# Loading and scaling the last segment's rows some slots sooner in both attention stages, and the second transform's last rows later

## The chip, the cores and the metric

The kernel runs on one core of a Trainium2 chip. The metric is the device time of one execution in microseconds (us). A core has a matrix engine (PE, TensorE), a vector engine (DVE), an activation engine (ACT), a general engine (POOL, GpSimd) and a queue engine (SP) that issues most DMA transfers. Each engine works through its own list of instructions in order; semaphores make one engine wait for another.

## The reference

Four layers follow each other on an activation of 2048 rows by 512 columns, each with a layer norm ahead of it and its result added to the row stream: a Fourier transform, an attention, the same Fourier transform, the same attention.

```python
x = A_x
x = x + _A_ref(_layernorm(x), dft_seq_re, dft_seq_im, dft_hid_re, dft_hid_im)
x = x + _B_ref(_layernorm(x), wq, wk, wv, wo, beta)
x = x + _A_ref(_layernorm(x), dft_seq_re, dft_seq_im, dft_hid_re, dft_hid_im)
x = x + _B_ref(_layernorm(x), wq, wk, wv, wo, beta)
```

`_layernorm` takes from each row its mean and divides by the root of its variance. `_A_ref` multiplies the rows by the DFT matrices along the hidden dimension and along the sequence, and keeps the real part. `_B_ref` has 32 heads of 16 columns and cuts the 2048 rows into 4 segments of 512; within a segment it is causal softmax attention, and earlier segments come in through a running memory that is read with the queries of a segment and updated with its keys and values.

## The kernel before

Rows are handled in 16 tiles of 128 (`NT`), four to a segment (`LT`), and segment `s` of an attention stage has tiles 4s to 4s+3. Four stages are laid out one behind the other on one axis of numbered slots: transform one at `a1`, attention one at `b1`, transform two at `a2`, attention two at `b2`. Every piece of work is a Python generator, and `place(order, gen, slots)` (L184) says in which slots its next step is traced; within a slot the steps go by `order` and then by the order in which they were placed. That trace is the program order.

PE instructions keep the program order (`in_order`, L78), and so do those wrapped in `pin`. For DVE, ACT, POOL and SP a planner makes each engine's list when the kernel is built: it steps through a modelled time and takes the earliest in program order among what it holds to be ready, so a later step can be drawn ahead into a gap. The row maxima of the scores (L827) are marked more urgent than their place. `behind_max` (L161) keeps an instruction behind the maximum that was traced last.

Layer norm of a tile is a chain over three engines. `moments` (L130) takes mean and variance on DVE (bn_stats L132, bn_aggr L133), `inverse_roots` (L140) adds epsilon on DVE (L143) and raises to the power -0.5 on POOL (L145), `row_scale` (L148) refines that in four small DVE instructions (L150 to L153), and `normal` (L164) makes the scaled rows `xn` on DVE (L166). For most tiles the statistics are taken by the stage that makes the rows (`measure`, L199). Only the last segment's tiles 12 to 15 lack them, so the next stage must take them itself.

In an attention stage `prep` (L679) handles two tiles. Its steps are: load the two tiles (L680); for the last segment, take the statistics up to the POOL power (L685); for the last segment `row_scale` (L688), and `xn` of the first tile; four PE transposes of the first tile into `xnT` and the split of the result into `xT` (L695 to L699); `xn` of the second tile; its transposes. The segment's first pair is placed round the slot b-60 and its second round b-55 (L1190), where b is the segment's first slot. A unit of attention (four heads of one segment) takes ten slots, and a segment 80. In the same slots PE computes the scores of a unit (`nat` for the maxima, `sT` for the softmax, `pv_bank` with the values), projections (`pqk`, `pvv`) and the output product of an earlier segment (`po`).

In transform two, `normalise` (L210) handles two tiles in three steps at t-8, t-3 and t (L601): load; statistics, for tiles 12 to 15 alone; `row_scale`, `xn`, and the split of `xn` into `xa` on ACT (L96) and DVE (L98). The slots t stand in the list at L1250. PE multiplies `xa` with blocks of the DFT matrix, and each block (a "right") must be split too: `one_right` (L338) by one ACT and one DVE pass into a tile `chi` or `clo`, of which there are three each, four slots before its product; some blocks are first added to another on DVE (L444, L457). A product step is six matmuls in one slot. The second transform runs products P1 and P7 for two slots a step up to slot a2+56, then P7, P2 and P4 for three slots a step up to a2+80. Tiles 12 to 15 are first used from a2+69 on. `negate` (L642) writes `minus`, the sign-changed row scales of all 16 tiles, for `add_rows` (L253), which scales and adds rows for the last products from slot a2+80 on.

Tiles loaded by `load_rows` share five buffers (`xt`, L119) and the `xn` tiles two. SP issues the loads in its own list, among the block fetches, the stack loads of the units and the writes of results.

Of the kernel before, what the change touches and what calls it, by code (L numbers as in the profile page):

```python
# [14 lines left out]
ALU = mybir.AluOpType  # L15
# [6 lines left out]
NSEG = 4  # L22
L = S // NSEG
NT = S // P
DT = D // P
TC = S // 512
LT = L // P
# [29 lines left out]
def spectral_infini_kernel(  # L57
# [13 lines left out]
    V, A, G, T = nc.vector, nc.scalar, nc.gpsimd, nc.tensor  # L71
# [46 lines left out]
    def load_rows(src, name="xt"):  # L118
        t = sb.tile([P, 512], F32, name=name, tag="xt", bufs=5)  # L119
        nc.sync.dma_start(t, src)  # L120
        return t
# [26 lines left out]
    def row_scale(rr, ve, r):  # L148
        t = sb.tile([P, LT], F32, name="rt", bufs=2)[:, : rr.shape[1]]
        V.tensor_tensor(out=t, in0=r, in1=r, op=ALU.mult)  # L150
        V.tensor_tensor(out=t, in0=t, in1=ve, op=ALU.mult)
        V.tensor_scalar(t, t, -0.5, 1.5, op0=ALU.mult, op1=ALU.add)
        V.tensor_mul(rr, r, t)  # L153
# [30 lines left out]
    def place(order, gen, *at):  # L184
        for t in itertools.chain(*at):
            slots.setdefault(t, []).append((order, gen))

    def run_from(t, n, step=1):
        return range(t, t + n * step, step)
# [6 lines left out]
    row_r = consts.tile([P, NT], F32, name="row_r")  # L196
    minus = consts.tile([P, NT], F32, name="minus")
# [7 lines left out]
    def place_spectral(x_in, x_out, t0, end, ln_at, direct):  # L205
# [396 lines left out]
        t = start  # L602
        if direct:
            place(2, contract(0), run_from(t, 4 * HALF, 2))
            for k in range(HALF):
                place(3, read_plain(0, k), [t + 8 * k + d for d in (-12, -4, 1, 4)])
                place(3, change_rows(k), [t + 8 * k + d for d in (5, 9)])
            t += 8 * HALF
            names = "P1", "P2", "P7", "P4"
            for tcn in range(1, TC):  # L610
                for n, name in enumerate(names):
                    place(2, product(tcn, name), run_from(t + n, HALF, 4))
                for k in range(HALF):
                    place(3, read_all(tcn, k), [t + 4 * k + d for d in (-11, -6, -4, -2, -1)])
                t += 4 * HALF
            for k in range(HALF):
                place(3, join_rows(k), [t + 5 * k + d for d in (-33, -27)])
            for tcn in range(1, TC):
                for n, name in enumerate(CHAIN):
                    place(2, product(tcn, name), run_from(t + n, HALF, 3))  # L620
                for k in range(0, HALF, 2):
                    place(3, read_rest(tcn, k), [t + 3 * k + d for d in (-12, -6, -3, 0)])
                t += 3 * HALF
        else:
            SOLO = 1
            phases = [(("P1",), range(SOLO)), (("P1", "P7"), range(SOLO, TC)), (("P7", "P2", "P4"), range(SOLO)), (("P2", "P4"), range(SOLO, TC))]
            for names, tcns in phases:
                n = len(names)
                for tcn in tcns:
                    for j, name in enumerate(names):  # L630
                        place(2, product(tcn, name), run_from(t + j, HALF, n))
                    for k in range(HALF):
                        u = t + n * k
                        if n == 1:
                            place(3, read_one(tcn, k, "P1"), [u - 9, u - 4])
                        else:
                            first = n - 2
                            if first:
                                place(3, read_added(tcn, k), [u + d for d in (-10, -6, -4)])
                            place(3, read_pair(tcn, k, names[first:]), [u + first + d for d in (-10, -6, -4, -3)])  # L640
                    t += n * HALF
            def negate():  # L642
                V.tensor_scalar(minus, row_r, -1.0, None, op0=ALU.mult)
                yield

            place(3, negate(), [t - 50])
            for k in range(HALF):
                place(3, add_rows(k), [t - 48 + 6 * k, t - 44 + 6 * k])
            for tcns in (0, 1), (2, 3):
                at = {tcn: [] for tcn in tcns}  # L650
                for name, tcn in itertools.product(CHAIN, tcns):
                    at[tcn] += run_from(t, HALF)
                    for k in range(HALF):
                        place(3, read_one(tcn, k, name), [t + k + d for d in (-9, -4)])
                    t += HALF
                for tcn in tcns:
                    place(2, chained(tcn), at[tcn])
        for k in range(2 * DT):
            cc, d = k // DT, k % DT
            tag = "craw" if k < 2 else ("chi", "clo")[k % 2]  # L660
            t = end - 7 + k if k < 2 else end - 3 + (k - 2) // 2
# [13 lines left out]
    def place_attention(x_in, x_out, t0, w_at, out_at):  # L675
# [3 lines left out]
        def prep(s, n):  # L679
            xt = [load_rows(x_in[s * LT + i]) for i in n]  # L680
            yield
            mine = slice(s * LT + n[0], s * LT + n[-1] + 1)
            mv, rr = row_mv[:, mine], row_r[:, mine]
            if s == NSEG - 1:
                ve, r = row_stats(xt, mv)  # L685
            yield
            if s == NSEG - 1:
                row_scale(rr, ve, r)  # L688
            for j, i in enumerate(n):
                with behind_max():  # L690
                    xn = normal(xt[j], mv[:, j], rr[:, j : j + 1])
                yield
                if i == 0:
                    xT[s] = sb.tile([P, 2, DT, 512], F32R, name="xT", bufs=1)
                pt = bank("xnT", (P, DT, P))  # L695
                for d in range(DT):
                    T.transpose(pt[:, d], xn[:, d * P : (d + 1) * P], ident)
                sl = slice(i * P, (i + 1) * P)
                split(xT[s][:, 0, :, sl], xT[s][:, 1, :, sl], pt)  # L699
                if j + 1 < len(n):  # L700
                    yield
            yield
# [477 lines left out]
        for n in range(NSEG * USEG):  # L1180
            t = t0 + SU * n
# [5 lines left out]
        for s in range(NSEG):  # L1187
            b = t0 + SS * s
            for j in range(2):
                t = b - (43, 51, 60, 60)[s] + 5 * j  # L1190
                first = (8, 5, 3)
                place(2, prep(s, (2 * j, 2 * j + 1)), [*(t - d for d in first), t, t, t + 2])
            place(2, values(s), *([light(b - 20), light(b)] if s else [run_from(b - 18, 8), light(b - 10)]))
            place(2, alloc_out(s), [b - 13])
            o = b + SS
            if s < NSEG - 1:
                free = light(o + 20) + light(o + 40) if s < NSEG - 2 else run_from(o + 20, DT * LT, 3)
            else:
                free = [out_at(k) for k in range(4 * LT)]
            if s == NSEG - 1 and x_out is out_tiles:  # L1200
                for i in range(LT):
                    place(2, outproj_split(s, i), [o - 12 + i], range(o - 7 + 3 * i, o - 7 + 3 * i + 3) if i < LT - 1 else (o + 2, o + 4, o + 4), [o + 5 + 1, o + 7])
                place(1.5, transpose_last(s), [o + 5])
            else:
                for i in range(LT):
                    at = free[DT * i : DT * (i + 1)]
                    place(2, transpose_out(s, i), [at[0] - 4 - i % 2])
                    place(2, outproj(s, i), at)
            for g in range(NG):
                t = b + SG * g  # L1210
                late = [] if s or g > 1 else [b + 3 + 2 * g]
                at = {
                    (0, 0): run_from(b - 34, 8),
                    (0, 1): run_from(b - 26, 8),
                    (0, 2): among(b, b + 13, 8),
                    (0, 3): among(b + 13, b + 29, 8),
                    (1, 0): among(b - 40, b - 29, 8),
                    (1, 1): among(b - 29, b - 17, 8),
                }.get((s, g), light(t - 50))
                place(2, proj(s, g, "q"), at[:4], post(at[3]))  # L1220
                place(2, proj(s, g, "k"), at[4:], post(at[7]), late)
                if s > 0:
                    place(2, mem_read(s, g), [t - 12, t - 8])
                if s < NSEG - 1:
                    place(2, mem_update(s, g), [t + 6, t + 9] if g else [t + 16, t + 19])
# [10 lines left out]
    a2 = b1 + LB - 18  # L1236
    b2 = a2 + TC * 7 * HALF + LEAD

    def w_at(b):
# [7 lines left out]
    place_attention(mids[0], mids[1], b1, w_at(b1), lambda k: b1 + LB + 11 + k // 2)  # L1247
    place_spectral(
        mids[1], mids[2], a2, b2 - LEAD,
        [((2 * j, 2 * j + 1), a2 + t) for j, t in enumerate((-40, -24, -8, 2, 24, 34, 46, 54))],  # L1250
        False,
    )
    place_attention(mids[2], out_tiles, b2, w_at(b2), lambda k: b2 + LB + 8 + k)
# [83 lines left out]
```

## Time and profile before

| | |
|---|---|
| median of 3 runs | 1813.44 us (1812.06 to 1814.43) |
| profiled execution | 1812.16 us, span of its instructions 1810.4 us |
| PE busy | 1745.1 us, 96% of the span, 10192 matmuls |
| DVE busy | 1404.3 us, 78% |
| ACT busy | 1116.3 us, 62% |
| POOL busy | 475.7 us, 26% |
| mean granted PE clock | 0.994 of full speed |

Busy time is the time in which an engine has an instruction in work, and a matmul's end is modelled. A timeline row gives start, duration, engine, line, operation, output and inputs; where the engine sat idle before it, the idle time and what ended it stand in brackets at the end. Nearly all PE instructions have the line of one helper (L82), so they are told apart by the name of what they write. A row of time slices gives the busy time of PE, PE's weight loads, DVE, ACT and POOL in that slice, with the number of instructions in parentheses, and after them the granted PE clock (1.00 is full speed), the DMA share and GB/s.

### The profile page before, as it was taken

Reading aid. Unit: us, or ns where it says so; the run is one execution under the profiler, and the core shown is the slowest. Engines: PE = TensorE matmul, PEld = TensorE weight load, DVE = VectorE, ACT = ScalarE, POOL = GpSimd, SP = SyncE. Lnnn points to the kernel's source line nnn. Section 1 sums busy time; section 2 is a strip of 40 time slices with the busy share of each in tenths; the row PEclk is TensorE's granted clock in tenths of the full one; section 3 lists DMA queues with packets and bytes.
Section 4 is the critical chain, followed back from the end, with each engine's and each line's share of the span. In section 5 each row is a group of like instructions: output and inputs, shape, how many; then the busy total and the mean of one; then the engine's idle time right before and its main releaser. Section 6 shows DMA issues by size and latency. Waiting matters only on the chain.

```text
span 1810.4 us, 32184 instructions
## 1 busy us (share of the span) xinstructions
PE 1745.1 (96%) x10192; PEld 1260.2 (70%) x10192; DVE 1404.3 (78%) x4233; ACT 1116.3 (62%) x2391; POOL 475.7 (26%) x797
## 2 busy tenths in 40 slices
PE   7999999999999999999999999999998999999998
PEld 6888777877556666665578788888875666666654
DVE  8888987764877878878877997667658788787785
ACT  3334443432877878778764765444338887867785
POOL 1000000013443445355520000000134443534442
PEclk9999999999999999999999999999999999999999
DMA  8787765355443543444566876644545344344341
GB/s 279 245 274 236 249 228 169 116 168 175 137 151 108 156 127 123 138 127 132 164 205 203 275 231 221 195 147 153 170 136 179 124 138 144 116 138 139 103 130 42
DMA packets 169498, 302.81 MB, mean 167 GB/s; under 512 B 19568, under 2 KB 70768, under 8 KB 169328
## 3 DMA queue, kind: packets, MB, share of 16 engines
q1 hardware_dynamic: 159152, 287.39, 50.0%
q10 hardware_dynamic: 10176, 13.37, 2.0%
q8 instruction: 80, 1.31, 0.3%
q14 instruction: 90, 0.74, 0.1%
HBM read 211.83 MB, written 88.08 MB: 166 GB/s over the span
## 4 chain that ended last, share of the span: by engine, by line
PE 82%; DVE 10%; DMA 3%; issue 2%; ACT 2%; POOL 0%; SPq 0%; ACTq 0%; DVEq 0%; POOLq 0%
PE m L82 25%; PE pqk L82 9%; PE y L82 8%; PE pv_bank L82 8%; PE sT L82 7%; PE nat L82 6%; PE u L82 5%; PE pvv L82 4%; PE po L82 4%; DVE junk L827 3%; DVE c L520 1%; DVE clo L98 1%; PE on L82 1%; PE pm L82 1%; PE pM L82 1%
## 5 line engine op out<-in xcount | busy, mean ns | idle before, releaser
L827 DVE CUSTOM_DVE_ANT_0 junk<-nat,mask 128x512 bf16<-128x512 f32 (+3 forms) x1024 | 496.8, 485 | 159.6 <-PE nat L82 124.7
L896 ACT ACTIVATE pT<-sT 128x512 f32<-128x512 f32 x640 | 372.1, 599 | 14.7 <-DVE sT L893 1.4
L899 POOL TENSOR_SCALAR_AFFINE_SELECT pT<-pT 128x256 f32<-128x256 f32 (+1 forms) x448 | 199.1, 458 | 470.5 <-ACT pT L896 364.1
L82 PE MATMUL m<-chi,xa 128*128 128x512 f32 x1056 | 309.9, 394 | 5.6 <-ACT chi L96 2.7
L82 PE MATMUL sT<-stkq,stkk 99*128 99x256 bf16 (+3 forms) x1024 | 248.7, 304 | 3.9 <-ACT pT L896 1.6
L82 PE MATMUL nat<-stkk,stkq 96*128 96x512 bf16 (+3 forms) x1024 | 244.9, 300 | 6.8 <-DVE mx L827 3.4
L82 PE MATMUL m<-clo,xa 128*128 128x512 f32 x720 | 232.8, 396 | 4.1 <-DVE clo L98 4.1
L895 ACT ACTIVATE sT<-sT 128x256 f32<-128x256 f32 (+1 forms) x628 | 204.6, 336 | 49.3 <-PE sT L82 47.2
L82 PEld LDWEIGHTS m<-chi,xa 128*128 128x128 f32 x1056 | 198.7, 189 | 49.2 <-ACT chi L96 3.6
L82 PE MATMUL y<-wdt,us 128*128 128x512 f32 x768 | 182.3, 391 | 0.2 <-DVE wdt L98 0.2
L82 PEld LDWEIGHTS <-stkk 99*128 99x128 bf16 x1024 | 81.4, 98 | 132.1 <-issue 118.7
L82 PEld LDWEIGHTS y<-wdt,us 128*128 128x128 f32 x768 | 143.4, 188 | 30.4 <-DVE wdt L98 0.9
L82 PEld LDWEIGHTS m<-clo,xa 128*128 128x128 f32 x720 | 135.8, 189 | 36.2 <-DVE clo L98 8.3
L96 ACT ACTIVATE chi<-cring 128x512 fp32r<-128x512 f32 (+1 forms) x138 | 100.0, 728 | 95.7 <-PE m L82 42.6
L82 PE MATMUL pv_bank<-pT,v_all 128*17 128x128 f32 (+3 forms) x2048 | 154.0, 437 | 1.3 <-POOL pT L899 1.3
L145 POOL TENSOR_TENSOR r<-ve,half_neg 128x2 f32<-128x2 f32 (+2 forms) x24 | 19.4, 810 | 481.5 <-DVE ve L143 478.6
L82 PEld LDWEIGHTS <-stkq 96*128 96x128 bf16 x1024 | 94.1, 99 | 60.1 <-issue 19.0
L82 PE MATMUL pvv<-wv,xT 128*128 128x512 f32 x384 | 127.3, 443 | 3.7 <-DVE mx L827 3.7
L82 PE MATMUL pqk<-xT,wq 128*128 128x512 f32 x384 | 129.8, 447 | 0.0
L82 PE MATMUL po<-wo,oh 128*128 128x512 f32 x384 | 123.2, 436 | 3.1 <-DVE mx L827 2.2
L82 PE MATMUL pqk<-xT,wk 128*128 128x512 f32 x384 | 123.5, 430 | 0.0
L82 PEld LDWEIGHTS pv_bank<-pT,v_all 128*17 128x17 f32 x2048 | 53.5, 97 | 90.1 <-issue 83.9
(194 smaller groups left out, 2997.3 us busy)
## 6 DMA issues: line engine op xcount, KB each, us to landing
cring<-in_ct SPq DMA_DIRECT2D x97, 256.0 KB
stkq<-scrq SPq DMA_DIRECT2D x64, 384.0 KB
stkk<-scrk SPq DMA_DIRECT2D x64, 384.0 KB
cring<-sum SPq DMA_DIRECT2D x95, 256.0 KB
xt<-mid SPq DMA_DIRECT2D x64, 256.0 KB
cring<-in_ct SPq DMA_DIRECT2D x27, 512.0 KB
mid<-xr SPq DMA_DIRECT2D x48, 256.0 KB
scrq<-parts SPq DMA_DIRECT2D x32, 384.0 KB
```

The costliest lines, as they stand in the source:

```text
L82: return tc.keep_in_program_order(op(*args, **kwargs))
L96: pin(A.activation(hi, src, AF.Copy, scale=scale))
L98: lo_engine.tensor_tensor(out=lo, in0=src, in1=hi.bitcast(F32), op=ALU.subtract)
L145: G.tensor_tensor(out=r, in0=ve, in1=half_neg[:, :n], op=ALU.pow)
L520: V.tensor_tensor(out=dst, in0=c[tcn, base][:, m], in1=ps[m], op=op)
L827: last_max[0] = V.tensor_tensor_reduce(junk[:, :n], src, mask[:, 512 - n :], 1.0, 3e38, ALU.add, ALU.min, dst,)
L895: A.activation(blocks, blocks, AF.Relu)
L896: A.activation(dst, ps, AF.Exp, scale=-SCALE)
L899: G.affine_select(blocks, blocks, pattern=[[0, n] for n in blocks.shape[1:-1]] + [[1, P]], compare_op=ALU.is_ge, fill=0.0, base=0, channel ...
```

## The change

In both attention stages, the third of `prep`'s steps is cut in two for the last segment: `row_scale` gets a step of its own. The slots of that segment's steps become t-12 (load), t-10 (statistics), t-6 (`row_scale`) and t-3 (first `xn`), where they were t-8, t-5 and t-3 (`row_scale` and first `xn` together). The later steps at t, t and t+2 stay, and the other segments keep their slots.

In transform two, the last three pairs of tiles are normalised later: tiles 10 and 11 at a2+36 for a2+34, tiles 12 and 13 at a2+48 for a2+46, tiles 14 and 15 at a2+58 for a2+54, with their loads and statistics. `negate` is done in two parts: tiles 0 to 11 at t-60 and tiles 12 to 15 at t-36, where all sixteen were at t-50; t is a2+128 there.

```diff
-            def negate():
-                V.tensor_scalar(minus, row_r, -1.0, None, op0=ALU.mult)
+            def negate(some):
+                V.tensor_scalar(minus[:, some], row_r[:, some], -1.0, None, op0=ALU.mult)
                 yield
 
-            place(3, negate(), [t - 50])
+            place(3, negate(slice(0, NT - LT)), [t - 60])
+            place(3, negate(slice(NT - LT, NT)), [t - 36])
...
             if s == NSEG - 1:
                 row_scale(rr, ve, r)
+                yield
             for j, i in enumerate(n):
...
                 t = b - (43, 51, 60, 60)[s] + 5 * j
-                first = (8, 5, 3)
+                first = (12, 10, 6, 3) if s == NSEG - 1 else (8, 5, 3)
                 place(2, prep(s, (2 * j, 2 * j + 1)), [*(t - d for d in first), t, t, t + 2])
...
-        [((2 * j, 2 * j + 1), a2 + t) for j, t in enumerate((-40, -24, -8, 2, 24, 34, 46, 54))],
+        [((2 * j, 2 * j + 1), a2 + t) for j, t in enumerate((-40, -24, -8, 2, 24, 36, 48, 58))],
```

## The prediction

> **What bounds the kernel now.** I read the page's totals first, then what PE waits for, then the timeline round the longest of those waits.
>
> ```profile
> span 1810.4 us, 32184 instructions
> PE 1745.1 (96%) x10192; PEld 1260.2 (70%) x10192; DVE 1404.3 (78%) x4233; ACT 1116.3 (62%) x2391; POOL 475.7 (26%) x797
> ```
>
> PE is the bound, so only time in which PE stands still, or runs at a lower clock, can be won. The profiled execution took 1812.16 us, 1.73 beyond its span; the median of the runs is 1.28 above it. The view of waits on PE (total, times, longest) has at its head
>
> ```profile
> PE xnT L82 <- DVE xn L166: 10.2, 7, 2.2
> ```
>
> PE's timeline shows the longest of these seven waits, one in each attention stage, both before the first `xnT` of the last segment:
>
> ```profile
> 717.38 1.04 PE L82 MATMUL po<-wo,oh 128*128 128x512 f32 x3
> 720.58 0.63 PE L82 MATMUL xnT<-ident,xn 128*128 128x128 f32 x4 [2.16 <-DVE xn L166]
> ...
> 1607.86 0.63 PE L82 MATMUL xnT<-ident,xn 128*128 128x128 f32 x4 [2.15 <-DVE xn L166]
> ```
>
> A wait costs more than itself. Slices of 10 us (the third number from the end is the granted clock, the third busy time is DVE's):
>
> ```profile
> 700.00:710.00 10.00, 10.00 (x83) 6.27 (x82) 6.54 (x34) 6.92 (x16) 1.81 (x4) 1.00 0.29 80
> ...
> 720.00:730.00 10.00, 9.34 (x73) 5.89 (x73) 8.66 (x30) 5.78 (x13) 2.49 (x4) 0.83 0.46 146
> ...
> 1000.00:1010.00 10.00, 6.88 (x23) 4.95 (x22) 9.36 (x21) 7.88 (x14) 0.30 (x1) 0.83 0.66 214
> ...
> 1600.00:1610.00 10.00, 7.45 (x40) 5.01 (x40) 9.82 (x32) 7.11 (x18) 5.58 (x8) 0.95 0.65 197
> 1610.00:1620.00 10.00, 9.92 (x77) 6.05 (x76) 8.64 (x33) 7.03 (x17) 3.81 (x7) 0.88 0.39 125
> ```
>
> Behind each wait the clock falls: (1 - 0.83) x 10 = 1.7 us of clock lost at 720, (0.05 + 0.12) x 10 = 1.7 at 1600, and 1.7 at 1000. So each attention wait costs 2.16 + 1.70 = 3.86 us. A second reading gives a little more. The same `pvv` step, 80 slots apart:
>
> ```profile
> 576.97 0.97 PE L82 MATMUL pvv<-wv,xT 128*128 128x512 f32 x3 [0.41 <-DVE mx L827]
> 696.53 0.97 PE L82 MATMUL pvv<-wv,xT 128*128 128x512 f32 x3 [0.67 <-DVE mx L827]
> 820.59 0.96 PE L82 MATMUL pvv<-wv,xT 128*128 128x512 f32 x3 [0.76 <-DVE mx L827]
> ```
>
> The 80 slots that prepare segment 2 take 119.56 us, those of the last segment 124.06: 4.50 longer for nearly the same PE work.
>
> **The change in attention.** DVE's timeline in stage one, from the first pair's statistics to its `xn`:
>
> ```profile
> 710.75 0.69 DVE L132 BATCH_NORM_STATS2 st<-xt 128x6 f32<-128x512 f32 x1
> ...
> 714.59 0.16 DVE L143 TENSOR_SCALAR ve<-row_mv 128x2 f32<-128x2 f32 x1
> ...
> 716.43 0.61 DVE L150 TENSOR_TENSOR rt<-r 128x2 f32<-128x2 f32 x1
> ...
> 719.88 1.00 DVE L166 TENSOR_SCALAR xn<-xt,row_mv,row_r 128x512 f32<-128x512 f32 x2
> 720.80 0.69 DVE L132 BATCH_NORM_STATS2 st<-xt 128x6 f32<-128x512 f32 x1
> ```
>
> The chain takes 9.1 us from the first row to `xn`, with urgent maxima between its links. A slot is 119.56 / 80 = 1.49 us, so five slots more for the statistics (t-10 for t-5) are 7.5 us and three for the scale 4.5. `xn` keeps its place at t-3 but finds its scale ready. It then stands where the chain's first scale link stood, at 716.43 or sooner, and is done about 717; PE wants it at 717.38 + 1.04 = 718.42. So the wait of 2.16 goes with 1 us to spare. What makes room is DVE's idle time: 10 - 6.54 = 3.46 us in the slice from 700 to 710, for about 3.2 us of DVE work of the pair, an estimate: two statistics of 0.69, three small ones near 0.16, four scale links of 0.61 at most, less the overlap of one with the next. The second pair's statistics, which started at 720.80, come to where the first pair's were, so DVE between 710 and 718 has as much as before, and behind 720 about 3.2 less, in the place of the 3.86 that it had while PE stood. Without that room the same work would hold up a maximum and PE with it (the slower rival below). Segment 2 has the same slots without statistics, and there nothing on PE waits for `xn`:
>
> ```profile
> L82 PE MATMUL xnT<-ident,xn x16: 270/272/273, 598.2 to 610.5; 128*128 128x128 f32 x16
> ...
> who waited for it (us, times):
>   ACT xT L96: 0.4, 2
> ```
>
> The loads cost and win nothing: SP issues them long before either place.
>
> ```profile
> 641.44 0.33 SPq L120 DMA_DIRECT2D xt<-mid  x1
> ...
> 974.83 0.80 SPq L120 DMA_DIRECT2D xt<-mid  x2
> ```
>
> The last is out 69 us before 710.75; four slots are 6. They pass nothing on SP that waits for them. POOL's power moves with the statistics; POOL is busy 1.81 of the 10 us at 700, so the masks queued behind it have room. PE's own list is unchanged in every stage. Terms: -3.86 and -3.85; bounds for each, 0 to -4.5.
>
> **The clock, by the page.** Those 1.7 us follow waits of 2.16. The Trainium skill ("TensorE: Matmul & The Clock Gate", Part 1) says that the clock halves after an idle window of about 3.4 us; by that rule waits of 2.2 us would not lower it, and the sum would win 2.16 and 2.15 alone. The granted clock fell all the same, so the rows decide.
>
> **The change in transform two.** PE, ACT and DVE round the other wait:
>
> ```profile
> 989.76 1.43 PE L82 MATMUL m<-chi,xa 128*128 128x512 f32 x5 [0.39 <-DVE chi L98]
> ...
> 997.83 1.52 PE L82 MATMUL m<-chi,xa 128*128 128x512 f32 x6
> 999.19 1.52 PE L82 MATMUL m<-clo,xa 128*128 128x512 f32 x6
> 1003.43 0.49 PE L82 MATMUL m<-chi,xa 128*128 128x512 f32 x1 [2.73 <-ACT chi L96]
> ...
> 1008.54 1.54 PE L82 MATMUL m<-chi,xa 128*128 128x512 f32 x6
> ```
>
> ```profile
> 1001.71 1.15 ACT L96 ACTIVATE xa<-xn 128x512 fp32r<-128x512 f32 x2 [4.45 <-DVE xn L166]
> ```
>
> ```profile
> 989.02 0.68 DVE L98 TENSOR_TENSOR chi<-cring,chi 128x512 fp32r<-128x512 f32 x1
> ...
> 993.83 0.69 DVE L132 BATCH_NORM_STATS2 st<-xt 128x6 f32<-128x512 f32 x1
> ...
> 1002.05 0.17 DVE L643 TENSOR_SCALAR minus<-row_r 128x16 f32<-128x16 f32 x1
> ...
> 1003.59 0.69 DVE L98 TENSOR_TENSOR chi<-cring,chi 128x512 fp32r<-128x512 f32 x1
> 1004.19 0.69 DVE L457 TENSOR_TENSOR craw<-craw,cring 128x512 f32<-128x512 f32 x1
> ```
>
> A block is split four slots before its product, and both waits come four slots behind a pair's last step: the ACT split of `xa` waits 4.45 us for `xn`, and the `chi` behind it is late. A product step takes 999.19 - 997.83 = 1.36 us. From 999.19 to 1008.54 PE does three in 9.35 us where three are 4.08, so 5.27 us are lost there (a wait of 2.73, one of 0.4 in the middle of that step, and the clock), with 0.39 at 989.76.
>
> Is it only the place, or too much DVE work? From the first block behind tiles 12 and 13 (989.02) to the first behind 14 and 15 (1003.59) DVE had 14.57 us of work, for 8 slots of PE, 10.9: 3.7 short. After the change there are 10 slots, 13.6 us. The two more slots bring 5 passes in 3 slots (two additions, three splits) of 0.60 each (1003.59 to 1004.19), 2.0 us; the sign change of 0.17 can leave: 16.4, 2.8 short. The pair before moves two slots too, in a stretch with 3 passes in 2 slots, which gains 2.7 - 1.8 = 0.9 of lead and so covers its own 0.39, and up to 0.5 of the next wait. I expect 2.3 to 2.8 us of wait for the 2.73 + 0.4 of now, and the clock to fall as it does after 2.16. The term is 0.4 + 0.6 = -1.0. Bounds: -5.7 if nothing waits any more. For the loss: the first sign change no longer needs tiles 12 to 15, so the planner can draw `add_rows` ahead of their chain. Its passes are
>
> ```profile
> 1007.80 0.42 DVE L261 TENSOR_TENSOR xn<-xn 128x256 f32<-128x256 f32 x1
> ```
>
> three of 0.42 and two splits of 0.4 and 0.7 at most, near 1.9 us beside a second stretch of low clock, 1.7: +3.6. The extra sign change is one more instruction of 0.17 at most, in DVE's idle time before 975 or beside PE. The loads of tiles 14 and 15 went out by 974.83, 19 us before 993.83; four slots (5.4 us) later they still lead, and let block fetches pass. If that cover fails, two issues cost 0.80. I take 0.
>
> **Sum.** 1812.16 - 3.86 - 3.85 - 1.0 = 1803.45; with 1.28 to the median, **1804.7 us**.
>
> **The rivals.** (1) *The transform's wait goes whole*: -7.7 - 5.7 = 1798.8, on the median 1800.0. For it: the chain leaves the place where it shares DVE with the end of a product. Against it: DVE's 2.8 us too much. 0.13.
>
> (2) *Attention waits only shrink*, since `xn` stays behind the urgent maxima. Segment 1 of stage one has no statistics either and yet waits 1.38:
>
> ```profile
> 500.32 0.38 PE L82 MATMUL nat<-stkk,stkq 96*128 96x512 bf16 x1 [1.36 <-DVE mx L827]
> ...
> 505.23 0.63 PE L82 MATMUL xnT<-ident,xn 128*128 128x128 f32 x4 [1.38 <-DVE xn L166]
> ```
>
> 0.8 each is won, with or without the clock: -2.6 to -6.0 with the transform's 1.0, 1807.5 to 1810.9. 0.11.
>
> (3) *Slower: the earlier statistics make a maximum late.* PE then waits before `nat`, as at 500.32, and `xnT` still waits behind. There both waits and a longer low clock cost
>
> ```profile
> 500.00:510.00 10.00, 7.35 (x38) 4.46 (x38) 8.62 (x37) 7.70 (x19) 2.34 (x6) 0.82 0.52 168
> 510.00:520.00 10.00, 10.00 (x74) 5.81 (x73) 6.03 (x29) 5.60 (x15) 2.08 (x5) 0.84 0.17 46
> ```
>
> 1.36 + 1.38 + 3.4 = 6.1, and 7.0 with small ones. In the place of 3.86 in both stages that is +6.3, less 1.0: 1818.7. It decides once the moved work exceeds DVE's 3.46 us of room before the pair; 3.2 leaves little, but segment 2 speaks against it. 0.09.
>
> (4) *It doesn't do what it says*: the planner leaves the chain where it was. Loads run 69 us ahead of their slot, so slots do not rule there; but the statistics stayed at 710.75 with their data long there and DVE idle before, so on DVE they do. 1813.4. 0.05.
>
> (5) *Low clock stays, elsewhere*: only the waits go, -2.16 - 2.15 - 1.0, 1808.1. The gate rule of the Trainium skill named above would lead there. Against it: in these slices the clock falls right behind a wait. 0.04.
>
> (6) *Transform worse by its bound*, attention as forecast: -7.7 + 3.6, 1809.3. 0.05.
>
> **How the numbers follow.** The forecast has 0.53, its own range 1801.5 to 1808. A measurement can tell about 0.2%, 3.6 us, from no change, so faster is below 1809.8 and slower above 1817.1. Faster: 0.53 + 0.13 + half of (2) and most of (5) and (6), 0.76. Same: (4) and the rest of (2), (5), (6), with a little of (3), 0.15. Slower: 0.09. The range from 1799.5 to 1811 holds all but (3) and (4).
>
> **What would show it.** Right: no wait of PE for `xn` above 0.7 near 718 and 1600, full clock there, 80 slots of the last segment in about 120 us, statistics before 706, and a wait of 2 to 3 us with one low clock stretch near 1000. Wrong: new PE waits for `mx` between 695 and 730, `xn` still late, or `add_rows` passes on DVE ahead of the statistics of tiles 14 and 15 with a longer wait there.

## The result, and the profile after

The changed kernel took 1804.12 us (median of 4 runs) where the kernel before, timed beside it, took 1813.58: a ratio of 0.9945 [0.9923, 0.9966]. A second timing, told again below, gave 1805.89 us (5 runs) against 1813.92, ratio 0.9955 [0.9943, 0.9968]. One of the four executions of the changed kernel took 8212 us and is left out of the ratio; the median of the other three is 1803.65. So by the two ratios the change is 8 to 10 us faster (5.8 to 14 by their intervals), and the forecast of 1804.7 was met. The profiled execution took 1803.65 us. Its page begins:

```profile
span 1801.9 us, 32171 instructions
PE 1740.9 (97%) x10192; PEld 1259.7 (70%) x10192; DVE 1404.6 (78%) x4234; ACT 1114.7 (62%) x2391; POOL 476.6 (26%) x797
```

PE has the same 10192 matmuls in the same order. The work on the other engines is the same too, with one more instruction on DVE, though its order may differ; only PE's waits and its clock can differ. In the view of waits on PE (total, times, longest) the two longest of the seven waits for `xn` are gone:

```profile
PE xnT L82 <- DVE xn L166: 5.8, 5, 1.7
```

PE's timeline has the first `xnT` of the last segment without a wait, in both stages, and the step `pvv` 80 slots apart:

```profile
714.25 0.60 PE L82 MATMUL xnT<-ident,xn 128*128 128x128 f32 x4
...
1600.91 0.60 PE L82 MATMUL xnT<-ident,xn 128*128 128x128 f32 x4
```

```profile
692.49 0.96 PE L82 MATMUL pvv<-wv,xT 128*128 128x512 f32 x3 [0.67 <-DVE mx L829]
...
812.69 0.97 PE L82 MATMUL pvv<-wv,xT 128*128 128x512 f32 x3 [0.76 <-DVE mx L829]
```

The last segment's 80 slots now take 120.20 us, 3.86 less than the 124.06 before. DVE's timeline shows the chain of the first pair, with its scale ready 9 us before `xn`:

```profile
698.46 0.69 DVE L132 BATCH_NORM_STATS2 st<-xt 128x6 f32<-128x512 f32 x1
...
701.61 0.16 DVE L150 TENSOR_TENSOR rt<-r 128x2 f32<-128x2 f32 x1 [0.82 <-POOL r L145]
...
702.20 0.16 DVE L153 TENSOR_TENSOR row_r<-r,rt 128x2 f32<-128x2 f32 x1
...
711.57 0.60 DVE L166 TENSOR_SCALAR xn<-xt,row_mv,row_r 128x512 f32<-128x512 f32 x1
```

In transform two there is one wait for `chi`, four product slots later than before:

```profile
1004.09 3.39 PE L82 MATMUL m<-chi,xa 128*128 128x512 f32 x6 [2.54 <-ACT chi L96]
```

The slices of 10 us have two lowered ones behind it, and the clock stays full where the two attention waits were (the third number from the end is the granted clock). It is not full everywhere: near 845, which the change does not touch, it falls where the kernel before, in its first profile, kept it at 1.00.

```profile
710.00:720.00 10.00, 9.61 (x82) 6.36 (x81) 9.72 (x33) 8.13 (x18) 6.36 (x8) 1.00 0.74 216
720.00:730.00 10.00, 9.92 (x64) 7.77 (x63) 9.86 (x39) 8.28 (x20) 3.16 (x8) 1.00 0.48 148
840.00:850.00 10.00, 7.37 (x38) 4.70 (x42) 8.24 (x28) 6.00 (x15) 5.70 (x9) 0.83 0.34 112
1000.00:1010.00 10.00, 7.37 (x20) 5.18 (x19) 8.74 (x20) 7.26 (x13) 0.69 (x1) 0.69 0.64 212
1010.00:1020.00 10.00, 10.00 (x45) 8.21 (x44) 9.92 (x19) 7.22 (x14) 0.00 (x0) 0.97 0.96 320
1600.00:1610.00 10.00, 9.92 (x85) 6.88 (x83) 9.72 (x38) 9.21 (x20) 4.56 (x7) 1.00 0.77 241
```

Since PE's order is the same everywhere, two traces can be laid over each other matmul by matmul. The table gives, for single profiles, the time between the same two matmuls of PE (found by their count; the times on top are those of the first profile before). "Again" are further profiles of the same two kernels, from the experiments.

| stretch (us in the profile before) | before | before again | after | after again | after, timed run |
|---|---|---|---|---|---|
| 497.36 to 516.93 | 19.6 | 16.2 | 16.1 | 18.8 | 18.8 |
| 714.40 to 726.03, first `xnT`, stage one | 11.6 | 11.6 | 7.7 | 7.7 | 7.7 |
| 843.20 to 861.38 | 18.2 | 22.2 | 21.9 | 21.9 | 21.8 |
| 973.03 to 1017.63, transform two | 44.6 | 44.6 | 44.7 | 43.2 | 43.3 |
| 1603.36 to 1613.23, first `xnT`, stage two | 9.9 | 9.8 | 5.9 | 5.9 | 5.9 |
| span | 1810.4 | 1811.2 | 1801.9 | 1807.2 | 1804.2 |

The two attention rows are firm: 11.6 against 7.7 and 9.9 against 5.9 in these five profiles, 7.9 us together. The runs below repeat them: 7.7 and 5.9 in all four other profiles with the attention edit, 11.6 or 11.7 and 9.9 in those that keep the old attention slots, but for one row of 8.3 (the run with the loads alone) and the smaller dose, which changes these slots in another way. Rows one and three move by 3 to 4 us between profiles of one and the same kernel. In the first pair of profiles they happened to cancel (-3.5 and +3.7); they are no work of the change.

### The profile page after: what moved, and what is told of

Same layout as the page of the kernel before. It is cut to its first block, busy times and chain, and to the rows that moved or that the text cites. A ratio compares the mean times of both kernels' runs of the same rounds, so it can differ in the third digit from the quotient of the medians.

```text
span 1801.9 us, 32171 instructions
## 1 busy us (share of the span) xinstructions
PE 1740.9 (97%) x10192; PEld 1259.7 (70%) x10192; DVE 1404.6 (78%) x4234; ACT 1114.7 (62%) x2391; POOL 476.6 (26%) x797
## 4 chain that ended last, share of the span: by engine, by line
PE 84%; DVE 10%; issue 2%; ACT 2%; DMA 2%; SPq 0%; POOL 0%; ACTq 0%; DVEq 0%
PE m L82 26%; PE pqk L82 9%; PE y L82 8%; PE pv_bank L82 8%; PE sT L82 7%; PE nat L82 6%; PE u L82 5%; PE po L82 4%; PE pvv L82 4%; DVE junk L829 3%; DVE c L520 1%; DVE clo L98 1%; PE on L82 1%; PE pM L82 1%; PE pm L82 1%
## 5 line engine op out<-in xcount | busy, mean ns | idle before, releaser
L82 PE MATMUL pv_bank<-pT,v_all 128*17 128x512 f32 (+3 forms) x2048 | 152.4, 434 | 0.8 <-POOL pT L901 0.8
L145 POOL TENSOR_TENSOR r<-ve,half_neg 128x2 f32<-128x2 f32 (+2 forms) x24 | 19.4, 809 | 481.9 <-DVE ve L143 479.8
```

The costliest lines, as they stand in the source:

```text
L82: return tc.keep_in_program_order(op(*args, **kwargs))
L145: G.tensor_tensor(out=r, in0=ve, in1=half_neg[:, :n], op=ALU.pow)
```

## The experiments

**The attention edit alone.** The transform's slots and its sign change stay as before.

```diff
             if s == NSEG - 1:
                 row_scale(rr, ve, r)
+                yield
...
-                first = (8, 5, 3)
+                first = (12, 10, 6, 3) if s == NSEG - 1 else (8, 5, 3)
```

> The attention part alone; transform two as before. Theory A (the forecast's steps): the two waits of 2.16 and 2.15 before the first xnT of the last segment and the 1.7 us of low clock behind each carry the gain, so this is 7.7 us faster than the kernel before (1805.8 on its median of 1813.5), the whole of what the full change won within 2 us. Theory B (the gain is shared): the full change's trace is 3.7 us ahead already at 512 us and loses 4 near 845, both outside the changed slots; if these come from the change through the planner, the attention part alone wins something else, below 5 or above 10 us.

Measured: 1806.61 us (12 runs) against 1812.69, ratio 0.9964 [0.9950, 0.9978], that is 4.0 to 9.1 us faster. Both waits for `xn` of the last segment are gone. The wait for `chi` stays as in the kernel before:

```profile
713.04 0.60 PE L82 MATMUL xnT<-ident,xn 128*128 128x128 f32 x4
...
994.38 0.50 PE L82 MATMUL m<-chi,xa 128*128 128x512 f32 x1 [2.71 <-ACT chi L96]
...
1596.97 0.60 PE L82 MATMUL xnT<-ident,xn 128*128 128x128 f32 x4
```

By time alone the interval reaches below the 5 us of theory B. The profile decides: its two stretches take 7.7 and 5.9 us, as with the full change. So this edit carries what the change gains.

**The transform's edits alone.**

```diff
-            place(3, negate(), [t - 50])
+            place(3, negate(slice(0, NT - LT)), [t - 60])
+            place(3, negate(slice(NT - LT, NT)), [t - 36])
...
-        [((2 * j, 2 * j + 1), a2 + t) for j, t in enumerate((-40, -24, -8, 2, 24, 34, 46, 54))],
+        [((2 * j, 2 * j + 1), a2 + t) for j, t in enumerate((-40, -24, -8, 2, 24, 36, 48, 58))],
```

> The later rows and the two-part sign change alone; attention as before. Theory A: DVE's surplus of 2.8 us stays, so the wait only moves to the product step four slots behind the new place, about 2.5 us with low clock behind it; time within 2 us of before (the forecast's term was -1.0, the trace of the full change says 0). Theory B (the transform part carries gain): 3 us or more faster. The waits of 2.16 and 2.15 in attention stay in both.

Measured: 1815.62 us (12 runs) against 1812.69, ratio 1.0013 [0.9999, 1.0026]: 0 to 4.7 us slower, and no gain. The waits for `xn` stay (2.16 in both stages), and that for `chi` is moved and a little shorter:

```profile
716.31 0.72 PE L82 MATMUL xnT<-ident,xn 128*128 128x128 f32 x4 [2.16 <-DVE xn L166]
...
1008.73 0.50 PE L82 MATMUL m<-chi,xa 128*128 128x512 f32 x1 [2.54 <-ACT chi L96]
```

**Both kernels once more**, unchanged, to see which differences of the first two profiles repeat.

> The kernel before once more, for a second trace. If the wait of nat near 500 us with its long low clock and the end of the attention stage near 845 us vary from run to run, this trace shows another sum at one of these places (3 to 4 us apart) with the same instruction order; if they belong to the program, it repeats 1.36 and 1.38 with 3.4 us of low clock at 500, and no wait above 1 us near 845.

> The changed kernel once more, for a second trace. If the wait of 3.0 us of mT near 842 us and its low clock are chance, this trace lacks them and is 4 to 5 us shorter there; if they belong to the program, they return. In both cases no wait of PE for xn above 0.7 us at the last segment, and a wait of 2 to 3 us near 1004.

Measured: 1812.94 and 1808.95 us in one profiled execution each. The kernel before, profiled again, has the wait near 845 that only the changed kernel had in the first pair, and full clock at 500, where its first profile showed 0.82:

```profile
847.56 0.22 PE L82 MATMUL mT<-ident_b,mparts 128*80 128x128 bf16 x1 [3.02 <-DVE mx L827]
```

```profile
500.00:510.00 10.00, 7.24 (x47) 4.38 (x48) 9.42 (x40) 8.85 (x22) 2.35 (x6) 1.00 0.61 185
```

What follows: both places vary from one execution to the next. Of these differences only the two attention waits separate the kernels in every profile.

**Only the loads sooner.** The last segment's loads go out four slots sooner; the scale has its own step but keeps its slot, and statistics and transform are untouched.

```diff
                 row_scale(rr, ve, r)
+                yield
...
-                first = (8, 5, 3)
+                first = (12, 5, 3, 3) if s == NSEG - 1 else (8, 5, 3)
```

> The kernel before, with only the loads of the last segment's rows four slots sooner in both attention stages; statistics, scale and transform two as before. Theory (the rows have been there for tens of us, the wait is for VectorE's order): the waits of 2.16 us for xn at about 716 and 1610 us stay as they are, time unchanged, 1810 to 1815 us. Rival (the rows come late): the waits shrink, 1804 to 1808.

Measured: 1809.8 us in one run, within the range of the kernel before beside it (1808.63 to 1817.87). Both waits are there at their old size, 2.16 and 2.15:

```profile
716.45 0.63 PE L82 MATMUL xnT<-ident,xn 128*128 128x128 f32 x4 [2.16 <-DVE xn L166]
```

So by the waits the sooner loads change nothing by themselves; a single time can't show a small gain or loss.

**A smaller dose.** Statistics and scale one slot sooner each, the scale in its own step, loads and transform as before.

```diff
                 row_scale(rr, ve, r)
+                yield
...
-                first = (8, 5, 3)
+                first = (8, 6, 4, 3) if s == NSEG - 1 else (8, 5, 3)
```

> The kernel before, with the last segment's statistics and its scale one slot sooner each in both attention stages, scale in a step of its own, row loads where they were, transform two untouched. Theory (the wait for xn is 2.16 us plus some 1.7 us of low clock and needs the row's xn 2.2 us sooner; one slot is 1.5 us): the wait shrinks to below 1 us or goes, and with it the low clock: 6 to 8 us faster, 1805 to 1807, as with the whole attention edit. Rival (a slot is not enough; the wait of 2.16 us shrinks to 0.6 to 0.7 us, and low clock stays): 3 to 4 us faster, 1809 to 1810.

Measured: 1817.74 us (10 runs) against 1813.53, ratio 1.0024 [1.0010, 1.0037], **slower** by 2 to 7 us. Neither theory holds. The wait grew in both stages, from 2.16 to 3.73 and from 2.15 to 3.72:

```profile
718.48 1.09 PE L82 MATMUL xnT<-ident,xn 128*128 128x128 f32 x4 [3.73 <-DVE xn L166]
```

DVE's timeline in stage one shows where the time went, with POOL's pass beside `xn` under it:

```profile
707.50 0.68 DVE L132 BATCH_NORM_STATS2 st<-xt 128x6 f32<-128x512 f32 x1
...
712.77 0.60 DVE L150 TENSOR_TENSOR rt<-r 128x2 f32<-128x2 f32 x1
...
715.07 0.68 DVE L132 BATCH_NORM_STATS2 st<-xt 128x6 f32<-128x512 f32 x1
...
716.27 0.15 DVE L153 TENSOR_TENSOR row_r<-r,rt 128x2 f32<-128x2 f32 x1
...
716.43 0.65 DVE L132 BATCH_NORM_STATS2 st<-xt 128x6 f32<-128x512 f32 x1
717.01 1.78 DVE L166 TENSOR_SCALAR xn<-xt,row_mv,row_r 128x512 f32<-128x512 f32 x2
```

```profile
716.90 1.15 POOL L768 TENSOR_TENSOR parts<-rem,parts 128x512 bf16<-128x512 f32 x1 [0.74 <-ACT parts L764]
```

PE wants the row at 718.48 - 3.73 = 714.75. The first pair's statistics start 7.25 us ahead of that; before they started at 710.75 for 718.42, 7.67 ahead. So against PE they did not get sooner at all. What did get sooner are the second pair's statistics: they stood behind the first pair's `xn` (720.80 behind 719.88) and now stand in front of it, two of 0.6 to 0.7 us in an engine that works in order. Even so, from its start to `xn` the chain took only 0.38 us longer (9.51 for 9.13). The largest part lies in `xn` itself: the first of the two took 1.33 us, beside that POOL pass, where it took 0.55 in the kernel before. So the 1.57 us that the wait grew are, to the rounding, 0.42 of a later start against PE, 0.38 of a longer chain and 0.78 of a slower `xn`; stage two has 0.39, 0.40 and 0.77. In the changed kernel the second pair's statistics stand in front of `xn` as well (706.73 and 708.02 for 711.57), but there the first pair's scale has been ready since 702.3.

**Rows 12 to 15 measured by the stage that writes them.** The changed kernel, with these statistics taken in attention one, as for the other rows.

```diff
-            known = not direct and n[-1] < NT - LT
+            known = not direct
...
-            if x_out is not out_tiles and s < NSEG - 1:
+            if x_out is not out_tiles:
                 measure(s, i, xr)
```

> The changed kernel, except that the statistics of rows 12 to 15 of transform two (mean, deviation and its inverse) are taken where attention one writes these rows, as for rows 0 to 11 already, and no longer in the transform's last two row steps. It takes four statistics of 0.66 to 0.68 us, four aggregates of 0.17 and two chains of about 2.6 us with their wait for GpSimd from VectorE between 978 and 1003 us, some 8 us. Theory (the wait of 2.54 us for chi at 1004 comes of VectorE's surplus of row work over these slots): the wait and both low-clock stretches behind it go, 5 to 6 us faster than the changed kernel, 1797 to 1800 us, ratio to the kernel before 0.992. Rival (the place of the rows against ScalarE's order holds the halves of chi up, whatever VectorE does): the wait stays at 2 to 3 us, 1803 to 1806. Second rival (the statistics now weigh on attention one's end, near 790 to 830 us): a new wait there, 1804 to 1808.

Measured: 1801.88 us (6 runs) against 1813.53, ratio 0.9949 [0.9929, 0.9968]; the profiled execution took 1797.92. No wait for `chi` is left, and ACT's `xa`, which waited 6.72 us for `xn` in the changed kernel, runs without one:

```profile
996.46 1.14 ACT L96 ACTIVATE xa<-xn 128x512 fp32r<-128x512 f32 x2
```

```profile
1000.00:1010.00 10.00, 10.00 (x46) 8.29 (x45) 10.00 (x20) 7.24 (x14) 0.00 (x0) 1.00 0.92 309
```

The stretch of transform two takes 38.5 us instead of 43.2 to 44.7, so the wait and its low clock cost 4.7 to 6.2 us there, about as expected. The measured time fell by less (1801.88 against 1804.12 and 1805.89; one of the six runs took 1810.98 at a mean granted clock of 0.944, where the others had 0.993 to 0.998), and the interval does not reach the 0.992 that was expected.

**The same, with the attention edit and the old slots in transform two.** Against the run with the attention edit alone:

```diff
-            known = not direct and n[-1] < NT - LT
+            known = not direct
...
-            if x_out is not out_tiles and s < NSEG - 1:
+            if x_out is not out_tiles:
```

> The attention edit alone with transform two's rows and sign change at the places of the kernel before, and the statistics of rows 12 to 15 taken in attention one as in the run with measured rows. If VectorE's surplus is the cause of the wait for chi near 995 to 1000 us in the kernel before, it goes here as well, and the later place of the rows is worth nothing: 1797 to 1800 us, within 1 us of the run with measured rows at the later place. If the later place matters by itself, a wait of 1 to 3 us stays near 995 and the time is 2 to 5 us above that run.

Measured: 1798.65 us (6 runs) against 1813.53, ratio 0.9918 [0.9904, 0.9932]. This is the fastest version found, 12 to 17 us below the kernel before, and its interval lies below that of the changed kernel in its longer timing ([0.9943, 0.9968]). Its stretch of transform two takes 38.6 us. So the later slots are not needed once the rows come measured. Whether they cost something beside it stays open: the medians are 3.2 us apart and the intervals just touch. The profiles show no difference in that stretch, and 0.5 us in the one behind it, to about 1104 (86.9 with the later slots, 86.4 here).

**Half of it.** The changed kernel, with only rows 12 and 13 measured in attention one. What it leaves out: the inverse deviation of rows 12 and 13 is not computed for transform two; what attention one left there is used.

```diff
-            known = not direct and n[-1] < NT - LT
+            known = not direct and n[-1] < NT - 2
...
-            if x_out is not out_tiles and s < NSEG - 1:
+            if x_out is not out_tiles and (s < NSEG - 1 or i < 2):
```

> The changed kernel with the statistics of rows 12 and 13 alone taken in attention one, those of 14 and 15 still in transform two: half of what the run with measured rows takes off VectorE. Theory (VectorE's surplus adds up over both row steps): 3.2 to 4 us less work ahead of the wait of 2.54 us for chi, so it shrinks below 1 us or goes; ratio to before 0.990 to 0.993. Rival (the last row step's own burst of some 6 us holds the chi's half up by itself): the wait stays at 2 to 2.5 us with low clock behind it, ratio 0.994 to 0.996.

Measured: 1806.69 us (4 runs) against 1813.92, ratio 0.9962 [0.9948, 0.9975], and a wait of 2.39 in the place of 2.54. This is what the rival expected. PE and DVE of this run:

```profile
1005.59 0.62 PE L82 MATMUL m<-chi,xa 128*128 128x512 f32 x1 [2.39 <-ACT chi L96]
```

```profile
994.49 0.69 DVE L520 TENSOR_TENSOR c<-c,m 128x512 f32<-128x512 f32 x1 [2.85 <-PE m L82]
...
1000.50 0.17 DVE L133 BATCH_NORM_AGGREGATE row_mv<-st 128x2 f32<-128x6 f32 x1
...
1005.73 0.68 DVE L98 TENSOR_TENSOR chi<-craw,chi 128x512 fp32r<-128x512 f32 x1
```

DVE sits idle for 2.85 us just ahead, so it is not short of time. But from 1000.50 to 1005.73 it does nothing but the row step of tiles 14 and 15, with 0.81 us of waiting for POOL's power in it, and no block is split on DVE in these 5.23 us. The changed kernel has the same stretch of the same length, and ACT is held up beside it:

```profile
999.01 0.17 DVE L133 BATCH_NORM_AGGREGATE row_mv<-st 128x2 f32<-128x6 f32 x1
...
1004.24 0.69 DVE L98 TENSOR_TENSOR chi<-craw,chi 128x512 fp32r<-128x512 f32 x1
```

```profile
1002.36 1.15 ACT L96 ACTIVATE xa<-xn 128x512 fp32r<-128x512 f32 x2 [6.72 <-DVE xn L166]
1003.42 0.61 ACT L96 ACTIVATE chi<-craw 128x512 fp32r<-128x512 f32 x1
```

ACT's half of the block stands behind `xa` in its queue though DVE had the block's sum `craw` (L444) ready at 997.9; DVE's half comes 0.8 us later. Both halves are held up by the same chain. Which of the two queues alone would be enough to make PE wait was not tried.

**The two transform edits apart**, and the changed kernel timed beside them.

The kernel with the later slots alone:

```diff
-        [((2 * j, 2 * j + 1), a2 + t) for j, t in enumerate((-40, -24, -8, 2, 24, 34, 46, 54))],
+        [((2 * j, 2 * j + 1), a2 + t) for j, t in enumerate((-40, -24, -8, 2, 24, 36, 48, 58))],
```

The kernel with the sign change alone (with `negate` taking a range, as in the change):

```diff
-            place(3, negate(), [t - 50])
+            place(3, negate(slice(0, NT - LT)), [t - 60])
+            place(3, negate(slice(NT - LT, NT)), [t - 36])
```

> The kernel before, with only the row steps of tiles 10/11, 12/13 and 14/15 of transform two 2, 2 and 4 slots later; one sign change at its old place, attention as before. Theory (the burst of VectorE's row work is moved, not made smaller): the wait for chi moves from about 1002 to about 1008 us, 2.5 to 2.8 us long, time 0 to 3 us above before. Rival (a later place gives the burst more room): wait below 2 us, 2 us faster.

> The kernel before, with only the sign change of the 16 rows split in two instructions at two places. One more instruction of 0.17 us on VectorE at most: 0 to 0.3 us, time that of before; the waits at 716, 1002 and 1610 us as before (2.16, 2.7, 2.15). If the sign change stood before something that the halves of chi wait for, the wait near 1002 goes with it: 2 to 5 us faster.

> The changed kernel itself, timed beside the two that follow on one chip, so that the transform's two edits can be taken off it. From the attention edit alone (about 6.5 us faster) and the transform's edit alone (about 2 us slower): 3 to 8 us faster than before, ratio 0.9955 to 0.9985. If the two edits help each other: ratio below 0.995.

Measured, against 1813.92: later slots 1815.95 us (11 runs), ratio 1.0013 [1.0002, 1.0023]; sign change 1813.37 (11 runs), 0.9999 [0.9989, 1.0009]; the changed kernel 0.9955, as told above. The sign change costs nothing that shows. The later slots move the wait and leave it at 2.54, and by the time they cost 0.4 to 4.2 us. The profiles show only part of it: the stretch of transform two takes 43.4 us with the later slots alone and 43.7 with both transform edits, against 44.6 before, and the one behind it, to about 1104, is 0.5 longer. Both profiles also have 6.8 us of half clock near 1396, where neither profile of the kernel before has any, and their stretch from 1300 to 1420 takes about 1.4 us more. But the profile of the sign change alone has the same there, and that kernel was no slower, so this does not settle it. Within the changed kernel no such cost is seen: it is not slower than the attention edit alone (0.9955 against 0.9964). That part stays open.

## Why the prediction was right, point by point

**The attention terms** (-3.86 and -3.85) were right in size and in cause: -3.86 by the 80 slots, 7.7 for 11.6 and 5.9 for 9.9 in the table. The price of a wait, itself and 1.7 us of low clock, held here, but it is the common case and not a rule: in one of the six profiles with the two old waits the second was followed by no low clock (below). The cross-check that gave 4.50 was the poorer reading.

**The room for the chain**: as the prediction had it, it lies in DVE's idle time near 700, and no new wait for a maximum of 0.3 us or more appeared between 693 and 731. The margin was larger than reckoned: `xn` was done at 712.2 and PE took it at 714.25, 2 us instead of 1. Two of the rivals, the slower one by late maxima and the one with waits that only shrink, fell here. But the smaller dose shows that slower was close by: one slot in the place of five makes the wait 1.6 us longer, and not by a late maximum. The rivals had none of the three parts that add up to it there.

**The loads**: nothing won or lost that shows, as forecast; the run with the loads alone kept both waits.

**The transform term** (-1.0) is the term that was not borne out by the time. The wait was forecast at 2.3 to 2.8 us in place of 2.73 + 0.4, with the 0.39 at 989.76 gone: 2.54 was measured, and the 0.39 is gone. In four of the five profiles with the later slots but with the rows still measured in the transform (both "again" columns of the changed kernel, and the two kernels with transform edits alone) the stretch is 0.9 to 1.4 us shorter. In the first profile after, it is 0.1 longer, since there the low clock went on for twice as long (below). Timed alone, the edits gave 0 to +4.7 us and not -1.0. So inside its own stretch the term was about right; as a term of the sum it was 1 us too favourable at least. It hardly mattered: 1812.16 - 3.9 - 3.9 + 0.1 is 1804.5 on the profile's own scale, and 1803.65 was measured there, with the rest in the stretches that vary. That the sum of the forecast on that scale, 1803.45, came within 0.2 us is luck: the stretches near 500 and 845 cancelled to 0.2 in this pair of profiles, and each can move by 3 to 4.

**Its reason was wrong.** "Too much DVE work", counted over all the work between two blocks, was the step that failed: the run with half of the rows measured has 2.85 us of idle DVE in that stretch and nearly the same wait, 2.39. The count also took as work 0.97 us in which DVE waited for POOL and ACT. What the rows show in its place is one run of row work of 5.23 us, about as long as the four slots (4 x 1.36 = 5.4 us) by which blocks are split ahead, with the splits on DVE and on ACT queued behind it. Taking the statistics out of this run took the wait away; that its length alone makes the wait is an argument. The forecast size came out by luck, since the count was not what sets it: the move left the gap between two splits on DVE nearly as long, 6.43 us from start to start (997.81 to 1004.24) for 6.70 (996.89 to 1003.59).

**The gate.** The prediction weighed the rule of the Trainium skill that it cites, and let the rows decide. That was right: with the waits went their low clock, 7.9 us and not the 4.31 of the waits alone.

**The rivals**: the transform's wait did not go whole by this change; measuring the rows elsewhere does that, and the price named for it (5.7) is what the stretch then gave (4.7 to 6.2). The rival by which the planner leaves the chain where it was fell with the first statistics, now at 698.46. Of low clock that stays elsewhere there is a trace: both further profiles of the changed kernel have 3.4 us of half clock near 1394, neither profile of the kernel before has any, but the stretch from 1300 to 1420 is about as long (119.8 and 120.5 us for 120.0 and 120.2).

## What to carry to other kernels

Here a step that waited for a chain over several engines was cured by taking the whole chain far ahead; moved by a little, it won nothing against PE, the neighbour's chain got in front, and the wait grew. A wait behind a burst on an in-order queue moved when the burst was moved, and went when the burst was made shorter, by taking the statistics where the rows are written. One pair of profiles can show differences of 3 to 4 us that belong to neither kernel; profile each twice before explaining them.

## What the runs showed of the hardware

**Low clock comes in stretches of one length, on a fixed grid.** Slices of 2 us behind the wait for `chi`, the changed kernel's first profile and then the one of its timed run:

```profile
1004.00:1006.00 2.00, 1.82 (x4) 1.12 (x5) 2.00 (x4) 2.00 (x5) 0.00 (x0) 0.50 0.60 231
1006.00:1008.00 2.00, 2.00 (x6) 1.61 (x5) 1.87 (x4) 2.00 (x5) 0.00 (x0) 0.50 0.78 222
1008.00:1010.00 2.00, 2.00 (x6) 1.51 (x6) 2.00 (x5) 1.63 (x3) 0.00 (x0) 0.50 0.86 306
1010.00:1012.00 2.00, 2.00 (x9) 1.61 (x8) 2.00 (x5) 0.91 (x3) 0.00 (x0) 0.84 1.03 351
```

```profile
1006.00:1008.00 2.00, 1.55 (x3) 1.01 (x4) 2.00 (x4) 2.00 (x5) 0.00 (x0) 0.60 0.62 218
1008.00:1010.00 2.00, 2.00 (x6) 1.55 (x5) 1.86 (x4) 2.00 (x5) 0.00 (x0) 0.54 0.84 215
1010.00:1012.00 2.00, 2.00 (x10) 1.65 (x9) 2.00 (x5) 1.64 (x3) 0.00 (x0) 1.00 0.96 290
```

Behind waits of 2.54 and 2.53 us the clock was at half for some 6.8 us in the one (3.0 + 0.16 x 2 us lost, and 0.1 just ahead) and for 3.4 in the other (0.40 x 2 + 0.46 x 2 = 1.7 lost). And the second wait of 2.15 us in the run with the loads alone was followed by none at all:

```profile
1600.00:1610.00 10.00, 7.46 (x51) 4.89 (x53) 9.78 (x33) 7.09 (x18) 5.59 (x9) 1.00 0.63 194
1610.00:1620.00 10.00, 9.87 (x84) 6.91 (x76) 9.75 (x37) 7.69 (x19) 4.01 (x9) 1.00 0.45 149
```

So in these runs a wait of 2.2 to 2.5 us cost itself and 0, 1.7 or 3.4 us more. The clock records in the traces say more than the slices. In all fourteen, each stretch of half clock but the one at the trace's end lasts 3.41 or 6.83 us, and within a trace the stretches begin whole multiples of 3.413 us apart. On the grid that they make, eleven of the twelve waits of 2.14 to 2.16 us for `xn` lie between two of its lines (to 0.02 us), and half clock begins at the next line. The twelfth is the one in the loads run: it is cut by a line into 0.30 and 1.85 us. So there it was the place of the wait on the grid, and not its length, that made the difference. Shorter waits can have it too: of 28 waits of 1.37 or 1.38 us near 500 and 1390, 11 had half clock at or right behind them. The Trainium skill ("TensorE: Matmul & The Clock Gate", Part 1) has the clock decided in free-running windows of about 3.4 us; stretches of one and two times that length agree. That a whole idle window is needed for the fall does not: 2.15 to 2.54 us of idle time were enough in most cases.

**Small DVE instructions stretch beside POOL work.** In the kernel before, the first scale link took 0.61 us at 716.43; in the changed kernel it took 0.16 at 701.61, where POOL did nothing until 704.59. In the kernel before POOL had this beside it:

```profile
715.86 1.16 POOL L767 TENSOR_TENSOR parts<-rem,parts 128x512 bf16<-128x512 f32 x1
```

Near 845, where profiles differ by 4 us, an instruction on 128x16 elements took 1.30 us in the kernel before's second profile and 0.16 in its first; beside the long one, POOL ran a pass of 1.26 that began 0.01 us later:

```profile
845.73 1.30 DVE L850 SCALAR_TENSOR_TENSOR mparts<-mrem,mparts 128x16 bf16<-128x16 f32 x1
```

```profile
845.74 1.26 POOL L98 TENSOR_TENSOR xa<-xn,xa 128x512 fp32r<-128x512 f32 x1
```

The Trainium skill ("SBUF — State Buffer", Who interferes with whom) says that a DVE instruction with two inputs in SBUF contends with a GpSimd instruction that reads SBUF, and that the port pair they share is an exclusive lock. The rows agree with that: the long one ends 0.03 us after POOL's. In the run with the sign change alone the same instruction met the same POOL pass, again 0.01 us ahead of it, and took 0.16:

```profile
846.01 0.16 DVE L851 SCALAR_TENSOR_TENSOR mparts<-mrem,mparts 128x16 bf16<-128x16 f32 x1
```

```profile
846.02 1.29 POOL L98 TENSOR_TENSOR xa<-xn,xa 128x512 fp32r<-128x512 f32 x1
```

```profile
846.70 0.22 PE L82 MATMUL mT<-ident_b,mparts 128*80 128x128 bf16 x1 [1.88 <-DVE mx L828]
```

There PE's wait near 845 was 1.14 us shorter than 3.02, as much as the instruction was, and no low clock followed. The instruction took 1.29 or 1.30 us in eleven of the fourteen profiles, whose stretch in the third row of the table takes 21.8 to 23.0 us, and 0.16 in the three others, with 18.1 to 19.4. This compares executions as they fell; no run set out to bring it about, and why the one race went the other way the traces don't show.
